# Mirrored filter rows by way of DRAM copies instead of flip products, no dummy root, first products from a constant

## The chip, the cores and the metric

The kernel runs on one core of a Trainium2 chip. The metric is the device time of one execution in microseconds (us). Inputs and output lie in DRAM; the work is done by TensorE (PE, matrix products, with its weight loads shown as PEld), VectorE (DVE), ScalarE (ACT), GpSimd (POOL, hardly used here) and SyncE (SP), which issues nearly all transfers (DMA).

## The reference

The input x (2048 x 512) goes two ways, and a gate mixes the results.

```python
x = A_x
g = _sigmoid((x * gate_w).sum(-1, keepdims=True))
a = irfft2(rfft2(x) * (w_r + 1j * w_i))          # 2048 x 512, filter 2048 x 257
h = layernorm(x)                                  # over the 512 columns
u = gelu(h^T @ w1 + b1)                           # 512 x 1792
b = (u @ w2 + b2)^T                               # 2048 x 512
return g * a + (1 - g) * b
```

`B_x` is not used. The part that the change is about is the product of the spectrum with the filter: the filter has 2048 rows (one for each frequency along the first axis) of 257 values, in a real half `A_w_r` and an imaginary half `A_w_i`. The kernel makes use of a symmetry between frequency k and frequency 2048 - k, so it needs each filter row together with its mirrored row in the same partition.

## The kernel before

**How the work is tiled.** The rows of x are held as 16 tiles of 128 rows (four blocks q, and within a block the row number modulo four, r). The transform is made of products with cosine and sine tables (L554 to L557 along the rows, L653 along the columns), with sums and differences on DVE between them (L566/L567, `radix4` at L585 to L601, L669 to L677). The spectrum lies in `X` and then in `B`, in two halves `lt`: the even frequencies (0) and the odd ones (1). It is multiplied by the filter (L820 to L842), taken back by the inverse products (L890 to L898, L967 to L970), and added to the other branch (L1017, L1024, L1030). The other branch is two dense products: L705 (with w1) sums over the 16 row tiles into one PSUM bank for each of 14 column tiles, gelu follows on ACT (L721), and L1011 (with w2) makes the 16 output tiles, each from 14 products. These 448 products of 512 columns are the bulk of PE's work; the short transform products stand between them.

**What sets the order.** Each piece of work is handed to a planner (`Plan`, L133) with its engine, its expected duration, a priority, the keys that it reads and writes, and, for loads, a size in bytes. `Plan.order` (L167) runs a small model of the engines and one model of the DMA (at most eight loads outstanding, 388 KB/us) and then emits all instructions in the order found. On the chip each engine works through its instructions strictly in this order, so a plan that expects a load too early makes its reader wait, and all that stands behind the reader on the same engine too. All transfers but five are issued by SP in one queue; each carries one of eight completion counters, in turn.

**The filter.** `W` (L325) holds, for each half (comp), each `lt` and four groups e, a forward row (s = 0) and its mirrored row (s = 1). `ld_W` (L433) loads one half in sixteen transfers: for `lt` = 1 the mirrored rows come by four transfers with a reversed source (L444), 128 rows each. For `lt` = 0 the rows that are to be mirrored are first loaded forward into a buffer `wt` (L439 to L442); PE then turns them over by products with a reversed unit matrix `flip` (`wf`, L757, and `wfn`, L767), and ACT copies the result into `W` (`wfe`, L761, and L770). Here is the core of the reversed load:

```python
for e in range(4):
    dma(W[:, 1, e, 1, 0:257], v[:, 3 - e, 3, :].rearrange("(o i) l -> o i l", o=4)[:, ::-1])
```

`wprep` (L775 to L782, DVE) halves one row of the filter and takes sums and differences of its end columns. It reads and writes all of `W`, so it runs after every load and every copy into it. `c0b` (L809 to L814) and the multiplications (L828) follow.

In SP's queue the order around the filter is: weights `wb` for column tiles 7 to 10, the tables, `ld_W(0)`, weights `wb` for tiles 11 to 13, `ld_W(1)`, then the w2 rows into `wa`.

**The start.** `alloc_first` (L308) allocates the buffers and clears a few of them on DVE, among them `warm`, the first 512 columns of `xp` (L317). PE multiplies this tile by itself ten times (`warm`, L356) ahead of the first real work. ACT takes the square root of a constant (`presq`, L361), which loads the table of the root. Then DVE takes the mean and variance of the first tile (L487, L488), ACT its root (L511), DVE the reciprocal and the normalised tile h (L516, L521), and PE starts with L705.

Of the kernel before, what the change touches and what calls it, by code (L numbers as in the profile page):

```python
# [264 lines left out]
def kernel(  # L265
# [23 lines left out]
    pool = ctx.enter_context(tc.tile_pool(name="sb", bufs=1))  # L289
    psum = ctx.enter_context(tc.tile_pool(name="ps", bufs=1, space=bass.MemoryType.PSUM))  # L290
# [17 lines left out]
    def alloc_first():  # L308
# [7 lines left out]
        t["warm"] = t["xp"][:, 0:D]  # L316
        V.memset(t["warm"], 0.0)  # L317
# [10 lines left out]
        t["wt"] = sb([P, 2, 4, WL], BF16, "wt")  # L328
# [12 lines left out]
    a0 = add("SP", 0.01, alloc_first, writes=["warm", "xs", "eps"], prio=-9)  # L341
# [11 lines left out]
    def warm():  # L353
        pw = ps([P, D], F32, "fa", 2)
        for _ in range(NWARM):
            T.matmul(pw[:], lhsT=t["warm"][:, 0:P], rhs=t["warm"], start=True, stop=True)  # L356
    NWARM = 10
    add("PE", 0.42 * NWARM, warm, reads=["warm", "xs"], writes=["warmed"], prio=-5, alloc=["fa"], free=["fa"])

    def presq():  # L360
        A.activation(t["ombb2"][:, 0:1], t["eps"][:], ActF.Sqrt, bias=t["eps"][:, 0:1], scale=1.0)  # L361
    add("ACT", 0.05, presq, reads=["eps"], writes=["omg"], prio=-5)


# [68 lines left out]
    def ld_W(comp):  # L433
# [3 lines left out]
        def emit():  # L437
            W, u = t["W"][:, comp], t["wt"][:, comp]
            dma(u[64:127, :, 0:257], v[65:128, :, 0, :])  # L439
            dma(u[0:64, :, 0:257], v[64:128, :, 2, :])  # L440
            dma(u[127:128, 0:2, 0:257], z[0:1, 1, 2:4, :])
            dma(u[127:128, 3:1:-1, 0:257], z[0:1, 0, 0:4:3, :])  # L442
            for e in range(4):
                dma(W[:, 1, e, 1, 0:257], v[:, 3 - e, 3, :].rearrange("(o i) l -> o i l", o=4)[:, ::-1])  # L444
# [4 lines left out]
            dma(W[0:1, 0, :, 0, 0:257].rearrange("w (u v) l -> w u v l", u=2), z[0:1, :, 0:2, :])  # L449
            dma(t["wn"][:, comp, 0:257], wsrc[comp][1024:1025, :])  # L450
        return emit

    for comp in range(2):
        add("SP", 12.3, ld_W(comp), writes=[("W", comp), ("wt", comp)], prio=17 + 8 * comp, nbytes=300000, after=[a0])
        if comp == 0:
            load_wb(1)
# [291 lines left out]

    for comp in range(2):
        for lt in (0,):  # L750
            for a in range(2):
                tag = ("fa", "fb")[a]

                def wf(comp=comp, lt=lt, a=a, tag=tag):
# [324 lines left out]
```

## Time and profile before

| what | us |
|---|---|
| median of three runs | 127.81 (127.77 to 128.35) |
| the profiled execution | 127.68 |
| its span | 125.9 |
| PE busy | 120.5 |
| DVE busy | 113.8 |
| ACT busy | 81.0 |
| first L705 product starts | 5.56 |
| filter loads issued by SP | 24.90 to 50.29 |
| flip products L757 | 38.7 to 53.6 |
| `wprep` (L777) starts | 57.46 |
| first L1011 product starts | 64.5 |

The profile shows one execution. Its span runs from the first to the last instruction; 1.78 us of the execution's time lie outside of it. The page gives, for each engine, its busy time and its share of the span, and below that the span in 40 slices of 3.15 us, a digit for each slice: 9 means busy for 90% or more. The groups give line, engine, operation, tiles and count, then the busy time in us and the mean duration of one in ns, then the idle time of that engine just before them and what ended it. In a timeline the first number is the start and the second the length; "SPq" is SP issuing a transfer. Products on PE overlap: the duration of one (379 ns for 512 columns) is longer than the distance from one start to the next (216 ns), and it is the distance that counts for a PE that is full. About two records in a hundred of PE's products are missing from the trace, so that a distance of twice 216 ns is mostly no gap.

### The profile page before, as it was taken

To read this page: it belongs to the slowest core of one execution; us is meant where nothing else is said; L and a number is where in the kernel's file an instruction comes from. 1 tells how busy PE (TensorE), PEld (TensorE's weight loads), DVE (VectorE), ACT (ScalarE), POOL (GpSimd) and SP (SyncE) were. 2 spreads that over 40 slices of the span, in tenths; PEclk is the share of its full clock that TensorE was granted. 3 is DMA by queue.
4 is the path that set the end of the run, shared out by engine and by line. 5 is a ranking of instruction groups with operands and counts; after the bars stand their busy time and mean duration, and the time that the engine had idled before them with its cause. 6 is when DMAs were issued, how large, how long until landed. Compare 5 with 4: busy or idle time off the path is not lost.

```text
span 125.9 us, 2138 instructions
## 1 busy us (share of the span) xinstructions
PE 120.5 (96%) x743; PEld 68.8 (55%) x756; DVE 113.8 (90%) x273; ACT 81.0 (64%) x165; POOL 0.2 (0%) x4
## 2 busy tenths in 40 slices
PE   6899999999999999999999999999999999999991
PEld 2344555555655476644445555555577767655590
DVE  2699999999999999999999999999988999999651
ACT  0973689699999999999420004722299999952200
POOL 0000000000000000000000000000000000000000
PEclk9999999999999999999999999999999999999999
DMA  1999999994459946799999900000000000006541
GB/s 57 305 371 358 382 365 358 348 315 86 117 119 288 268 86 162 210 413 411 410 408 407 389 25 0 5 0 0 3 0 0 0 5 0 0 21 229 200 180 44
DMA packets 18219, 23.12 MB, mean 184 GB/s; under 512 B 2190, under 2 KB 15904, under 8 KB 18208
## 3 DMA queue, kind: packets, MB, share of 16 engines
q1 hardware_dynamic: 17616, 22.36, 52.6%
q10 hardware_dynamic: 592, 0.62, 1.6%
q8 instruction: 6, 0.10, 0.3%
q14 instruction: 5, 0.04, 0.1%
HBM read 20.86 MB, written 2.10 MB: 182 GB/s over the span
## 4 chain that ended last, share of the span: by engine, by line
PE 73%; DMA 17%; SPq 7%; issue 1%; DVE 0%
PE acc L1011 32%; PE acc L705 20%; DMA wa<-in_B_w_dram 9%; SPq L306 7%; PE fb L1011 5%; DMA wt<-in_A_w_r_dram 5%; DMA x<-in_A_x_dram 3%; PE fb L653 2%; PE fa L653 2%; PE fa L890 2%; PE fb L890 1%; PE fb L705 1%; PE fa L967 1%; PE fb L967 1%; PE fa L1011 1%
## 5 line engine op out<-in xcount | busy, mean ns | idle before, releaser
L705 PE MATMUL acc<-h,wb 128*128 128x512 bf16 x108 | 25.9, 379 | 0.1
L1011 PE MATMUL acc<-gl,wb 128*128 128x512 bf16 (+1 forms) x94 | 23.9, 371 | 0.2
L1011 PE MATMUL acc<-gl,wa 128*128 128x512 bf16 (+1 forms) x97 | 23.8, 371 | 0.1
L1017 ACT ACTIVATE x<-acc,ombb,omg 128x512 bf16<-128x512 f32 x12 | 9.1, 782 | 21.2 <-PE acc L1011 21.2
L1011 PEld LDWEIGHTS <-wa 128*128 128x128 bf16 x126 | 13.5, 113 | 9.9
L1011 PEld LDWEIGHTS <-wb 128*128 128x128 bf16 x126 | 13.3, 113 | 9.3
L705 PE MATMUL acc<-h,wa 128*128 128x512 bf16 x62 | 17.3, 379 | 0.1
L705 PEld LDWEIGHTS <-wb 128*128 128x128 bf16 x112 | 10.7, 98 | 10.6
L705 PEld LDWEIGHTS <-wa 128*128 128x128 bf16 x112 | 10.3, 98 | 10.7 <-DMA wa<-in_B_w_dram 0.8
L487 DVE BATCH_NORM_STATS2 stats<-x 128x6 f32<-128x512 bf16 x14 | 9.5, 679 | 2.1 <-DMA x<-in_A_x_dram 2.0
L560 ACT CAST xp<-fa 128x512 bf16<-128x512 f32 x16 | 9.1, 581 | 1.8 <-PE fa L557 1.8
L735 ACT ACTIVATE x<-x 128x512 bf16<-128x512 bf16 x16 | 10.2, 691 | 0.0
L721 ACT ACTIVATE gl<-acc,b1f 128x512 bf16<-128x512 f32 x11 | 7.9, 718 | 3.2 <-PE acc L705 3.2
L705 PE MATMUL fb<-h,wa 128*128 128x512 bf16 x31 | 9.5, 379 | 0.1
L527 ACT ACTIVATE h<-x,nmr,rstd 128x512 bf16<-128x512 bf16 x11 | 8.4, 808 | 1.1 <-DMA wb<-in_B_w_dram 0.8
L705 PE MATMUL fa<-h,wa 128*128 128x512 bf16 x16 | 5.9, 378 | 0.7 <-DVE h L521 0.6
L653 PEld LDWEIGHTS <-X 128*128 128x128 bf16 x64 | 4.7, 98 | 2.1
L974 ACT ACTIVATE B<-fb,g 128x512 bf16<-128x512 f32 x8 | 5.7, 713 | 0.0
L974 ACT ACTIVATE B<-fa,g 128x512 bf16<-128x512 f32 x8 | 5.6, 705 | 0.1
L660 ACT CAST X<-fb 128x512 bf16<-128x512 f32 x8 | 5.1, 634 | 0.0
L660 ACT CAST X<-fa 128x512 bf16<-128x512 f32 x8 | 5.0, 620 | 0.0
L356 PE MATMUL fa<-xp 128*128 128x512 bf16 x10 | 3.8, 549 | 1.2 <-DVE xp L317 1.2
(169 smaller groups left out, 232.7 us busy)
## 6 DMA issues: line engine op xcount, KB each, us to landing
wb<-in_B_w_dram SPq DMA_DIRECT2D x11, 512.0 KB
wa<-in_B_w_dram SPq DMA_DIRECT2D x7, 512.0 KB
wa<-in_B_w_dram SPq DMA_DIRECT2D x2, 896.0 KB
wb<-in_B_w_dram SPq DMA_DIRECT2D x4, 384.0 KB
out_dram<-x SPq DMA_DIRECT2D x3, 512.0 KB
x<-in_A_x_dram SPq DMA_DIRECT2D x2, 512.0 KB
wa<-in_B_w_dram SPq DMA_DIRECT2D x2, 448.0 KB
rot<-dft_ti SPq DMA_DIRECT2D x1, 768.0 KB
```

Of the source, the lines that this page charges most:

```text
L306: (eng or nc.sync).dma_start(out=out_ap, in_=in_ap)
L487: V.bn_stats(out=t["stats"][:, j, :], in_=t["x"][:, j // 4, j % 4, :])
L527: add("ACT", 0.71, lambda j=j: A.activation(t["h"][:, j // 4, j % 4, :], t["x"][:, j // 4, j % 4, :], ActF.Identity, bias=t["nmr"][:, j:j ...
L560: add("ACT", act(512), lambda r=r, dq=dq: A.copy(xe(r)[:, :, :, dq, :], t["pa", r, dq][:]), reads=[("pa", r, dq)], writes=[("X", r, dq)], ...
L653: T.matmul(pb[:, k % 2, k // 2], lhsT=t["X"][:, lt, EX[e], c, k, :], rhs=tbl(k, c), start=True, stop=True)
L660: A.copy(t["X"][:, lt, EX[e]].rearrange("p c j l -> p (c j l)").rearrange("p (h c g b) -> p h c g b", h=2, c=2, b=2)[:, :, c], t["pb", lt, ...
L705: T.matmul(t["u", ft][:], lhsT=w[:, j // 4, j % 4, c * P:(c + 1) * P], rhs=t["h"][:, j // 4, j % 4, :], start=(j == jorder[0]), stop=(j == ...
L721: gelus.append(add("ACT", act(512, 1) , lambda ft=ft: A.activation(t["gl"][:, ft, :], t["u", ft][:], ActF.Gelu_apprx_tanh, bias=t["b1f"][: ...
L735: A.activation(t["x"][:, q, r, :], t["x"][:, q, r, :], ActF.Copy, accum_out=t["glog"][:, 4 * q + r:4 * q + r + 1])
L974: A.activation(eo_v(p)[:, n], t["i3", j][:], ActF.Copy, scale=t["g"][:, j:j + 1])
L1011: T.matmul(t["y", j, m][:, cs], lhsT=w[:, o, 512 * q + r:512 * q + 512:4], rhs=t["gl"][:, ft, cs], start=(ft == 0), stop=(ft == NFT - 1))
L1017: A.activation(tbuf(j).rearrange("p h d -> p (h d)"), t["y", j, 0][:], ActF.Identity, bias=t["ombb2"][:, j:j + 1], scale=t["omg"][:, j:j + 1])
```

## The change

Three things are changed.

1. The flip products, their evictions, the buffer `wt` and the loads into it are gone, and so are the four reversed loads of a half. Instead, for each half, two transfers copy the rows that are to be mirrored from DRAM to a DRAM buffer in reversed order (`ld_flip`: `fe` for the even, `fo` for the odd frequencies, 512 rows of 514 bytes each). Ten transfers load the forward rows and the few rows of partition 0 (`ld_nat`), and three fetch the mirrored rows from the DRAM buffers (`ld_mir`). The planner is told 1.1 us of issuing and 700000 bytes for `ld_flip`, 5.5 and 300000 for `ld_nat`, 1.6 and 500000 for `ld_mir`. `wprep` and the multiplications name the new key `("W~", comp)` of the fetched rows.
2. `presq`, the root of a constant, is gone. The first real root now carries the table load.
3. The ten first products read a constant tile of ones (one column, repeated) that POOL writes at the program's start, in place of the cleared piece of `xp`; the clear is gone, and the products wait for nothing on DVE.

The planner orders all work anew with these. SP's queue around the filter is now: tables, the four copies, the ten forward loads of half 0, the `wb` weights for tiles 11 to 13, the ten forward loads of half 1, the six fetches, then the w2 rows. `wprep` stands on DVE right behind L591 of the second half (`lt` = 1) and ahead of L669 and of L597/L598 of that half; before, thirty instructions stood between L591 and it.

```diff
+    dram = ctx.enter_context(tc.tile_pool(name="dram", bufs=1, space=bass.MemoryType.DRAM))
...
-        t["warm"] = t["xp"][:, 0:D]
-        V.memset(t["warm"], 0.0)
...
-        t["wt"] = sb([P, 2, 4, WL], BF16, "wt")
...
     def warm():
         pw = ps([P, D], F32, "fa", 2)
+        one = lambda n: nc.const_aps.tensor(1.0, [P, n], BF16)
         for _ in range(NWARM):
-            T.matmul(pw[:], lhsT=t["warm"][:, 0:P], rhs=t["warm"], start=True, stop=True)
+            T.matmul(pw[:], lhsT=one(P), rhs=one(D), start=True, stop=True)
     NWARM = 10
-    add("PE", 0.42 * NWARM, warm, reads=["warm", "xs"], writes=["warmed"], prio=-5, alloc=["fa"], free=["fa"])
-
-    def presq():
-        A.activation(t["ombb2"][:, 0:1], t["eps"][:], ActF.Sqrt, bias=t["eps"][:, 0:1], scale=1.0)
-    add("ACT", 0.05, presq, reads=["eps"], writes=["omg"], prio=-5)
+    add("PE", 0.42 * NWARM, warm, writes=["warmed"], prio=-5, alloc=["fa"], free=["fa"])
...
-    def ld_W(comp):
+    def ld_flip(comp):
+        ev = wsrc[comp].rearrange("(e m w) l -> w e m l", e=4, w=2)[0, :, P:2 * P, :]
+        od = wsrc[comp].rearrange("(g i k) l -> k g i l", i=32, k=4)[3]
+
+        def emit():
+            fe = t["fe", comp] = dram.tile([4, P, 257], BF16, tag=f"fe{comp}", name=f"fe{comp}")
+            fo = t["fo", comp] = dram.tile([16, 32, 257], BF16, tag=f"fo{comp}", name=f"fo{comp}")
+            dma(fe[:], ev[:, ::-1])
+            dma(fo[:], od[:, ::-1])
+        return emit
+
+    def ld_nat(comp):
         v = wsrc[comp].rearrange("(e c k) l -> c e k l", e=4, k=4)
         z = wsrc[comp].rearrange("(v u w) l -> w u v l", v=4, u=2)
 
         def emit():
-            W, u = t["W"][:, comp], t["wt"][:, comp]
-            dma(u[64:127, :, 0:257], v[65:128, :, 0, :])
-            dma(u[0:64, :, 0:257], v[64:128, :, 2, :])
-            dma(u[127:128, 0:2, 0:257], z[0:1, 1, 2:4, :])
-            dma(u[127:128, 3:1:-1, 0:257], z[0:1, 0, 0:4:3, :])
-            for e in range(4):
-                dma(W[:, 1, e, 1, 0:257], v[:, 3 - e, 3, :].rearrange("(o i) l -> o i l", o=4)[:, ::-1])
+            W = t["W"][:, comp]
             for o in range(4):
                 dma(W[32 * o:32 * o + 32, 1, :, 0, 0:257], v[96 - 32 * o:128 - 32 * o, :, 1, :])
             dma(W[1:64, 0, :, 0, 0:257], v[1:64, :, 0, :])
             dma(W[64:128, 0, :, 0, 0:257], v[0:64, :, 2, :])
             dma(W[0:1, 0, :, 0, 0:257].rearrange("w (u v) l -> w u v l", u=2), z[0:1, :, 0:2, :])
+            dma(W[0:1, 0, 0:2, 1, 0:257], z[0:1, 0, 0:4:3, :])
+            dma(W[0:1, 0, 3:1:-1, 1, 0:257], z[0:1, 1, 2:4, :])
             dma(t["wn"][:, comp, 0:257], wsrc[comp][1024:1025, :])
         return emit
 
+    def ld_mir(comp):
+        def emit():
+            W, fe, fo = t["W"][:, comp], t["fe", comp], t["fo", comp]
+            m = fe[:].rearrange("e (p two) l -> two p e l", two=2)
+            dma(W[:, 1, ::-1, 1, 0:257], fo[:].rearrange("(e o) i l -> (o i) e l", e=4))
+            dma(W[1:64, 0, ::-1, 1, 0:257], m[1, 0:63])
+            dma(W[64:128, 0, ::-1, 1, 0:257], m[0, 0:64])
+        return emit
+
+    FL = (16, 16.1)
     for comp in range(2):
-        add("SP", 12.3, ld_W(comp), writes=[("W", comp), ("wt", comp)], prio=17 + 8 * comp, nbytes=300000, after=[a0])
+        add("SP", 1.1, ld_flip(comp), writes=[("flp", comp)], prio=FL[comp], nbytes=700000, after=[a0])
+    for comp in range(2):
+        add("SP", 5.5, ld_nat(comp), writes=[("W", comp)], prio=17 + 8 * comp, nbytes=300000, after=[a0])
+        add("SP", 1.6, ld_mir(comp), reads=[("flp", comp)], writes=[("W~", comp)], prio=26 + comp, nbytes=500000)
...
-                def wf(comp=comp, lt=lt, a=a, tag=tag):
-                    pw = t["pw", comp, lt, a] = ps([P, 2, L], F32, tag, 2)
-                    for i in range(2):
-                        T.matmul(pw[:, i], lhsT=t["flip"][:], rhs=t["wt"][:, comp, 3 - 2 * a - i, 0:L], start=True, stop=True)
...
-                def wfe(comp=comp, lt=lt, a=a):
-                    A.copy(t["W"][:, comp, lt, 2 * a:2 * a + 2, 1, 0:L], t["pw", comp, lt, a][:])
...
-    def wfn():
...
-    add("DVE", 0.8, wprep, reads=[], writes=[("W", 0), ("W", 1), "wpm"] + wtk, prio=1)
+    add("DVE", 0.8, wprep, reads=[], writes=[("W", 0), ("W", 1), ("W~", 0), ("W~", 1), "wpm"], prio=1)
...
-            add("DVE", tt(4096), mul, reads=["xs", ("W", comp), ("W~", comp, lt)], writes=[("pp", "st")[comp]], prio=pr)
+            add("DVE", tt(4096), mul, reads=["xs", ("W", comp), ("W~", comp)], writes=[("pp", "st")[comp]], prio=pr)
```

More of the change, by code (lines that the diff above doesn't have):

```diff
@@ L339, in alloc_first @@
             t[name] = sb(shape, F32, name)
-    a0 = add("SP", 0.01, alloc_first, writes=["warm", "xs", "eps"], prio=-9)
+    a0 = add("SP", 0.01, alloc_first, writes=["xs", "eps"], prio=-9)
     def load(key, shape, dt, src, nbytes, prio=0.0):
@@ L747 @@
     add("SP", 0.2, ld_ti, writes=["ti"], prio=39, nbytes=754176, after=[pl.last_w["pa", r, dq] for r in range(4) for dq in range(4)])
[L749 to L752, printed above, removed]
-                def wf(comp=comp, lt=lt, a=a, tag=tag):
-                    pw = t["pw", comp, lt, a] = ps([P, 2, L], F32, tag, 2)
-                    for i in range(2):
-                        T.matmul(pw[:, i], lhsT=t["flip"][:], rhs=t["wt"][:, comp, 3 - 2 * a - i, 0:L], start=True, stop=True)
-                add("PE", mm(256, 256), wf, reads=[("wt", comp), "flip"], writes=[("pw", comp, lt, a)], prio=5, alloc=[tag])
-                def wfe(comp=comp, lt=lt, a=a):
-                    A.copy(t["W"][:, comp, lt, 2 * a:2 * a + 2, 1, 0:L], t["pw", comp, lt, a][:])
-                add("ACT", act(512), wfe, reads=[("pw", comp, lt, a)], writes=[("W~", comp, lt)], prio=3, free=[tag])
-    def wfn():
-        pw = t["pwn"] = ps([P, 4, 2], F32, "fa", 2)
-        for e in range(4):
-            T.matmul(pw[:, e], lhsT=t["flip"][:], rhs=t["wt"][:, :, 3 - e, 256], start=True, stop=True)
-    add("PE", mm(*[4] * 4), wfn, reads=[("wt", 0), ("wt", 1), "flip"], writes=["pwn"], prio=5, alloc=["fa"])
-    wtk = [("W~", comp, 0) for comp in range(2)]
-    add("ACT", 0.3, lambda: A.copy(t["W"][:, :, 0, :, 1, 256], t["pwn"][:].rearrange("p e k -> p k e")),
-        reads=["pwn"], writes=wtk, prio=3, free=["fa"])
     pbk = [("pb", lt, e, c) for lt in range(2) for e in range(4) for c in range(2)]
```

## The prediction

> **What bounds the kernel now.** I read the page's shares and slices first, then the groups kept apart by shape, the start, and the timelines of SP, DVE and PE around 24 to 58 us.
>
> ```profile
> PE 120.5 (96%) x743; PEld 68.8 (55%) x756; DVE 113.8 (90%) x273; ACT 81.0 (64%) x165; POOL 0.2 (0%) x4
> ...
> PE   6899999999999999999999999999999999999991
> ...
> DMA  1999999994459946799999900000000000006541
> ```
>
> PE is busy from the second slice to the last but one. From start to start its 512-column products take 0.216 us, the 256-column ones 0.109, the 128-column ones 0.056, and between 5.56 and 123 us no idle gap over 0.3 us is left. PE work is therefore the time; DVE is next, with one gap of 1.5 us near the end.
>
> ```profile
> L757 PE MATMUL fa<-wt,flip 128*128 128x256 bf16 x4 | 0.8, 272 | 0.0
> L757 PE MATMUL fb<-wt,flip 128*128 128x256 bf16 x4 | 0.8, 272 | 0.0
> L767 PE MATMUL fa<-wt,flip 128*128 128x2 bf16 x4 | 0.2, 165 | 0.0
> ```
>
> These are the products that go.
>
> ```profile
> 1.21 3.77 PE L356 MATMUL fa<-xp 128*128 128x512 bf16 x10 [1.21 <-DVE xp L317]
> ...
> 4.38 0.30 ACT L361 ACTIVATE ombb<-eps 128x1 f32<-128x1 f32 x1
> 4.58 0.28 ACT L511 ACTIVATE rstd<-mv,eps 128x1 f32<-128x1 f32 x1
> ...
> 5.56 0.38 PE L705 MATMUL fa<-h,wa 128*128 128x512 bf16 x1 [0.57 <-DVE h L521]
> ```
>
> The first real product waits for DVE, which waits for the first real root, which stands behind the dummy root.
>
> ```profile
> 24.90 2.56 SPq L306 DMA_DIRECT2D wt<-in_A_w_r_dram  x4
> 27.95 7.55 SPq L306 DMA_DIRECT2D W<-in_A_w_r_dram  x11
> ...
> 36.01 2.62 SPq L306 DMA_DIRECT2D wb<-in_B_w_dram  x4
> 38.68 2.54 SPq L306 DMA_DIRECT2D wt<-in_A_w_i_dram  x4
> 41.27 8.55 SPq L306 DMA_DIRECT2D W<-in_A_w_i_dram  x11
> 49.87 0.42 SPq L306 DMA_DIRECT2D wn<-in_A_w_i_dram  x1
> 50.40 3.30 SPq L306 DMA_DIRECT2D wa<-in_B_w_dram  x7
> ```
>
> SP takes about 0.57 us per issue, and no transfer is issued before the one eight places earlier has landed: issues at 27.95, 29.96, 44.00 and 45.57 follow such landings at 27.94, 29.94, 43.98 and 45.56. The filter is complete only at 52.0.
>
> ```profile
> 46.68 0.68 DVE L591 TENSOR_TENSOR X<-xp 128x1024 bf16<-128x1024 bf16 x1
> 47.55 0.69 DVE L669 TENSOR_TENSOR B<-X 128x1024 bf16<-128x1024 bf16 x1 [0.18 <-ACT X L660]
> ...
> 57.46 0.41 DVE L777 TENSOR_SCALAR W<-W 1x1028 bf16<-1x1028 bf16 x1
> ```
>
> Today `wprep` (L777 to L781), the first reader of the whole filter, runs at 57.46, over 5 us after the filter has landed.
>
> ```profile
> 50.83 0.39 PE L653 MATMUL fa<-tb,X 128*128 128x128 bf16 x4
> ```
>
> This is the first product that needs L597/L598 of the second half.
>
> **The change part by part.**
>
> *Products and evictions gone.* 8 x 0.109 + 4 x 0.02 = 0.95 us of PE, on the path as long as PE is full. ACT loses 4 x 0.65 + 0.34 = 2.9 us; PE and DVE cover it, so nothing. If ACT were the bound it would be a gain of up to 2.9.
>
> *Start.* Without the dummy root the real one starts when the statistics are ready (4.39) instead of 4.58: the table still loads at 3.08 to 4.36, since it stands ahead of the root's wait. Gain 0.15 to 0.19, say 0.15. The ten products begin some 0.3 us earlier (no wait for the clear); they end before the first h exists, so nothing, between -0.1 and +0.1. The lost DVE clear (0.27) falls into a 1.97 us wait.
>
> *The loads.* Per filter half, 16 transfers become 15: two that copy mirrored rows from DRAM into DRAM, ten forward ones, three that fetch the copies. The order is: four copies (both halves), ten forward loads, four weight loads (`wb`), ten forward, six fetches, then `w2`. Every packet is 514 bytes; their mean in the packet records of before is 36 ns (median 28).
>
> How many DMA engines carry a copy decides. The four odd mirrored loads of before (destination 128 partitions, source 4 reversed groups) each report only four engine ends, at 31.50, 32.77, 34.15 and 35.25 us for the last: 1.1 to 1.4 us for 32 packets, 34 to 43 ns each; in the second half 23 to 27. `fe` has the same shape (4 reversed groups), so I take four engines with 128 packets each; `fo` has 16 groups, so 16 engines with 32. No trace shows this with DRAM as destination.
>
> The Trainium skill's page DMA: Bandwidth & Descriptors (Why a DMA increments its semaphore by 16 and not by 1) says that the count is the largest number up to 16 that divides the slowest dimension of both sides, which gives 4 for fe; by it the spread-copy rival below falls away and the sum stays as it is.
>
> So the four engines get 128 + 32 + 128 + 32 = 320 packets. At 36 ns that is 11.5 us, from 28.9 (when these engines ran free before) to 40.4, landed at about 40.9. The eighth transfer behind the last copy, a two-packet forward load, is issued only then. Two small issues of 0.62 and the last of the ten follow, so `wb` starts at 42.8 instead of 36.01. The last `wb` took 9.5 us from the first issue in before (45.56), of which about 2 was backlog; I take 50.5. Behind that landing stand the eight last issues, 8 x 0.57 = 4.6, so the last fetch is issued by 55.1, and it lands 3.2 to 4.2 later (3.2 in before for the like load): **X = 58.7**, the landing of the last fetch.
>
> *The moved `wprep`.* In the changed order DVE runs it right behind L591 of the second half, at about 47.2, ahead of L669 and of L597/L598, which now queue behind a wait until X. DVE then needs 0.45 (wprep's tail) + 1.33 (L669 to L671) + 1.28 (L597, L598), and PE's product of 50.83 can start at X + 3.1. In the changed order four more 512-column products (0.87) stand before that product, and 0.51 of the removed ones stood behind it (0.44 ahead), so PE has 1.38 less to do after it. PE's end moves by X + 3.1 - 50.83 - 1.38 = X - 49.1. PE itself comes to it at 50.83 + 0.87 - 0.44 - 0.15 = 51.1; what PE and the start save before the wait only makes PE wait longer.
>
> X - 49.1 = 9.6. If X came before 47.2, no wait would be left and the change would give -0.95 - 0.15 = -1.1.
>
> *DVE lag.* DVE resumes X - 47.1 late, makes up 0.85 (wprep no longer at 57.46), and so lags PE by 1.15 more than before. In before, the inverse products start 0.2 to 0.4 us behind DVE's last writes (L601 ends at 92.94, its reader runs by 93.8). Between 0 and 1.15; I take 0.8.
>
> *The clock.* PE stands for X + 3.1 - 51.1 = 10.7 us. Before the first products the array was idle too, and they ran at 0.427 us until 4.17 us, 2.96 us long, at half rate: 1.48 us lost. Gaps of 0.3 to 0.7 us cost nothing of that kind. Between 0 and 1.5; the pause is nearer to the idle start, so 1.5.
>
> The Trainium skill's page TensorE: Matmul & The Clock Gate (Part 1: The HAM clock gate) gives a window of about 3.4 us both for falling to half rate and for rising again; an estimate by it is 1.7 us, and the sum would be 139.8. That the clock falls in a pause inside the kernel no trace here shows.
>
> *w2.* The first `wa` transfer moves from 50.40 to about 55.7, and seven at 1.28 us each land by 69; their first reader moves from 64.5 to about 75. Hidden; without the pause it would cost up to 5.
>
> **Sum.** 127.68 (the profiled execution: span 125.9 and 1.78 around it; median 127.81) + 9.6 + 0.8 + 1.5 = 139.6, say **139.5**.
>
> **Rivals.**
> - *The copies spread over 16 engines.* Then 4 x 32 packets take 4.6 us, the forward loads wait for nothing but SP, `wb` starts at about 37 and lands by 45.5, and X is 53.4: 127.68 + 4.3 = 132.0, up to 134.3 with lag and clock. For it: `fe`'s DRAM side is one unbroken run of rows. Against: the four-ended loads above. 18 in 100.
> - *DRAM to DRAM is slow.* Each packet crosses DRAM twice; at double the 40 ns the 320 packets take 25.6 us and X is 72.8: 127.68 + 23.7 + 2.3 = 153.7. 9 in 100.
> - *The fetches are in time, and it is faster.* From 30.7, when a slot for the third forward load comes free, 27 issues of 0.55 us and a landing of 2.6 give 48.2 if no copy and no `wb` holds a slot. X - 49.1 = -0.9: 126.6 to 126.8. It decides at X = 49.1. Against: the `wb` landings held SP at 44.00 and 45.57 already in before. 5 in 100, and 2 in 100 for an X so near 49 that nothing is seen.
> - The forecast, four engines at 23 to 50 ns: X 55 to 64, with or without the clock, 134.5 to 145: 66 in 100.
>
> **How the numbers follow.** 139.5 is the likeliest case's. 131.5 to 147 leaves out the faster and equal cases (7), the slow copies (9) and a little of the spread ones. Half a per cent is about what a measurement of this kernel tells from no change: faster 0.05, same 0.02, slower 0.93.
>
> **What would show it.** DVE idle at L767 to L771 of the changed file from 47 us on, ended by a transfer into W; copies into `fe` with four engine ends, 4 to 5 us apart; SP held at 31 to 41 us; PE idle from 51 us until 3 us after DVE resumes, then products at 0.427 us for about 3 us. The forecast is wrong if `fe` lands on 16 engines, if packets between DRAM and DRAM take far from 36 ns, or if the last fetch lands before 49 us.

## The result, and the profile after

The changed kernel takes **144.38 us** (median of six runs, 143.21 to 145.85) against 127.79 us in the six runs of the kernel before beside it: 1.126 times as long, 95% interval 1.121 to 1.131. Run again beside later experiments it took 146.01 us (ratio 1.140, interval 1.136 to 1.144), so differences of about 1% between runs of different groups mean nothing here. The medians are over all runs of a kernel; the ratios leave out those that took over 1.5% longer than its fastest.

The profiled execution took 145.41 us with a span of 143.5. The page of the changed kernel, shares and slices (each slice is now 3.59 us):

```profile
PE 123.5 (86%) x744; PEld 69.1 (48%) x744; DVE 113.4 (79%) x272; ACT 78.9 (55%) x159; POOL 0.2 (0%) x4
...
PE   7999999999999930001999999999999999999991
...
PEclk9999999999999996555599999999999999999999
DMA  3999999953954980799999574000000000004441
```

PE's row has a hole from 51 us on, and the clock's row is at half in it and behind it. The rest of PE's row is as full as before. The timeline of SP in the changed kernel (start and length of the issue, or of a run of issues with the waits between them):

```profile
25.18 0.75 SPq L307 DMA_DIRECT2D fe<-in_A_w_r_dram  x1
25.99 3.94 SPq L307 DMA_DIRECT2D fo<-in_A_w_r_dram  x1
29.98 0.84 SPq L307 DMA_DIRECT2D fe<-in_A_w_i_dram  x1
30.86 4.08 SPq L307 DMA_DIRECT2D fo<-in_A_w_i_dram  x1
34.98 7.99 SPq L307 DMA_DIRECT2D W<-in_A_w_r_dram  x9
...
43.47 2.62 SPq L307 DMA_DIRECT2D wb<-in_B_w_dram  x4
46.14 9.74 SPq L307 DMA_DIRECT2D W<-in_A_w_i_dram  x9
...
56.38 0.66 SPq L307 DMA_DIRECT2D W<-fo  x1
...
59.35 1.43 SPq L307 DMA_DIRECT2D W<-fe  x2
60.88 4.01 SPq L307 DMA_DIRECT2D wa<-in_B_w_dram  x7
```

The two copies into `fo` held SP for 4 us each. The first forward load went out at 34.98, where before had its first load into `W` at 27.95; the last fetch was issued at 60.19 and landed at 65.49. The timeline of DVE in the changed kernel, where `wprep` is L767 to L771, and below it that of PE:

```profile
46.88 0.68 DVE L605 TENSOR_TENSOR X<-xp 128x1024 bf16<-128x1024 bf16 x1
56.47 0.42 DVE L767 TENSOR_SCALAR W<-W 1x1028 bf16<-1x1028 bf16 x1 [8.90 <-issue]
62.72 0.19 DVE L770 TENSOR_TENSOR wpm<-W 128x16 f32<-128x16 bf16 x1 [5.83 <-DMA W<-fo]
65.57 0.19 DVE L771 TENSOR_TENSOR wpm<-W 128x16 f32<-128x16 bf16 x1 [2.66 <-DMA W<-fe]
...
66.94 0.68 DVE L611 TENSOR_TENSOR X<-st 128x1024 bf16<-128x1024 bf16 x1
```

```profile
50.39 1.24 PE L719 MATMUL acc<-h,wb 128*128 128x512 bf16 x5
67.68 0.61 PE L667 MATMUL fa<-tb,X 128*128 128x128 bf16 x4 [16.05 <-DVE X L611]
```

DVE finishes L605 at 47.6, meets `wprep`, and stands in it for 8.90 + 5.83 + 2.66 us until the last fetch is there. (The profile puts the first of the three down to "issue", that is to nothing that it shows; a load into `W` landed at 56.39, just before it ended.) L611, which PE wants at 51.6 us, is behind `wprep` in DVE's order, so PE stands for 16.05 us. This hole, and about 2 us for the half clock behind it, cover the 17.7 us between the two profiled executions: behind the hole PE runs without a gap of 0.25 us or more to the end.

### The profile page after: what moved, and what is told of

Its sections match the earlier page's. It is cut to its first block, busy times and chain, and to the rows that moved or that the text cites. A ratio compares the mean times of both kernels' runs of the same rounds, so it can differ in the third digit from the quotient of the medians.

```text
span 143.5 us, 2115 instructions
## 1 busy us (share of the span) xinstructions
PE 123.5 (86%) x744; PEld 69.1 (48%) x744; DVE 113.4 (79%) x272; ACT 78.9 (55%) x159; POOL 0.2 (0%) x4
## 4 chain that ended last, share of the span: by engine, by line
PE 51%; DMA 28%; SPq 17%; DVE 2%; issue 1%; DVEq 0%
PE acc L1001 28%; SPq L307 17%; PE acc L719 9%; DMA fe<-in_A_w_i_dram 8%; DMA wa<-in_B_w_dram 7%; DMA wb<-in_B_w_dram 6%; PE fb L1001 5%; DMA W<-fe 4%; DMA x<-in_A_x_dram 3%; PE fa L880 1%; PE fb L880 1%; PE fa L667 1%; PE fb L667 1%; PE fb L957 1%; PE fa L957 1%
## 5 line engine op out<-in xcount | busy, mean ns | idle before, releaser
L719 PE MATMUL acc<-h,wb 128*128 128x512 bf16 x112 | 26.8, 390 | 0.0
L1001 PE MATMUL acc<-gl,wb 128*128 128x512 bf16 (+1 forms) x98 | 24.2, 372 | 0.0
L1001 PE MATMUL acc<-gl,wa 128*128 128x512 bf16 (+1 forms) x98 | 23.8, 372 | 0.0
L1007 ACT ACTIVATE x<-acc,ombb,omg 128x512 bf16<-128x512 f32 x12 | 9.2, 788 | 20.2 <-PE acc L1001 20.2
L1001 PEld LDWEIGHTS <-wa 128*128 128x128 bf16 x126 | 13.4, 113 | 10.0
L719 PE MATMUL acc<-h,wa 128*128 128x512 bf16 x64 | 18.1, 388 | 0.0
L1001 PEld LDWEIGHTS <-wb 128*128 128x128 bf16 x126 | 13.3, 113 | 9.4
L667 PE MATMUL fa<-tb,X 128*128 128x128 bf16 x32 | 3.6, 242 | 16.1 <-DVE X L611 16.1
L719 PEld LDWEIGHTS <-wb 128*128 128x128 bf16 x112 | 11.0, 101 | 12.1 <-issue 0.8
L719 PEld LDWEIGHTS <-wa 128*128 128x128 bf16 x112 | 10.5, 99 | 10.9 <-issue 1.0
L749 ACT ACTIVATE x<-x 128x512 bf16<-128x512 bf16 x16 | 10.1, 666 | 0.0
L719 PE MATMUL fb<-h,wa 128*128 128x512 bf16 x32 | 9.7, 379 | 0.0
L767 DVE TENSOR_SCALAR W<-W 1x1028 bf16<-1x1028 bf16 x1 | 0.4, 420 | 8.9 <-issue 8.9
L719 PE MATMUL fa<-h,wa 128*128 128x512 bf16 x16 | 6.1, 392 | 0.2 <-DVE h L535 0.2
```

The lines of the kernel that those rows point to most:

```text
L667: T.matmul(pb[:, k % 2, k // 2], lhsT=t["X"][:, lt, EX[e], c, k, :], rhs=tbl(k, c), start=True, stop=True)
L719: T.matmul(t["u", ft][:], lhsT=w[:, j // 4, j % 4, c * P:(c + 1) * P], rhs=t["h"][:, j // 4, j % 4, :], start=(j == jorder[0]), stop=(j == ...
L749: A.activation(t["x"][:, q, r, :], t["x"][:, q, r, :], ActF.Copy, accum_out=t["glog"][:, 4 * q + r:4 * q + r + 1])
L1001: T.matmul(t["y", j, m][:, cs], lhsT=w[:, o, 512 * q + r:512 * q + 512:4], rhs=t["gl"][:, ft, cs], start=(ft == 0), stop=(ft == NFT - 1))
L1007: A.activation(tbuf(j).rearrange("p h d -> p (h d)"), t["y", j, 0][:], ActF.Identity, bias=t["ombb2"][:, j:j + 1], scale=t["omg"][:, j:j + 1])
```

## The experiments

In what follows X is the time at which the last fetch into `W` landed, read from the trace.

### Copies into fe on 16 engines (e1_spread)

```diff
-            dma(fe[:], ev[:, ::-1])
+            dma(fe[:].rearrange("e p l -> p e l"), ev.rearrange("e m l -> m e l"))
```

> The changed kernel, but the two copies into fe walk the 128 rows as their outer dimension and not the 4 groups, so that they can go over 16 DMA engines; bytes and packets (514 bytes) are the same. The reversal of these rows is left out, so fe holds them in forward order. Theory A (the copies make the last fetch late because four engines carry 320 packets each, and SP is held behind them): each copy into fe reports 16 engine ends and lands about 3 to 5 us after its issue, the long issues of the fo copies (3.94 and 4.08 us) fall below 1.5 us, the first forward load is issued by 29 (34.98 in the changed kernel), and the last fetch lands between 51 and 57 us (65.49). PE resumes 2.2 us after that landing, so the time is 145.4 less 8 to 14, less up to 2 for a clock that no longer falls: 130 to 137, I take 133. Rival B (packets from DRAM to DRAM, or SP writing 512 packets, are slow however many engines carry them): the last fetch stays at 63 or later and the time at 142 to 146.

Measured: 142.96 us (ratio 1.1215, interval 1.116 to 1.127), X = 61.65. Every copy now reported 16 engine ends, the issues of `fo` fell to 1.40 and 1.21 us and the first forward load went out at 29.65, much as theory A had it. But the two copies into `fe` landed 9.1 and 11.1 us after their issue, where theory A had 3 to 5, and the last copy landed at 39.58, only 1.9 us earlier than in the changed kernel (41.44). Rival B's time came true, if not quite its X of 63 or later. The reason is in the stretches of this run (for each stretch: its length, then busy time and count of PE, PEld, DVE, ACT, POOL, then the clock, the DMA engines' packet time as a share of the stretch, which passes 1 where packets of one engine overlap, and GB/s):

```profile
30.00:32.00 2.00, 2.00 (x13) 1.07 (x12) 2.00 (x4) 1.99 (x5) 0.00 (x0) 1.00 1.29 86
32.00:34.00 2.00, 2.00 (x18) 1.41 (x17) 2.00 (x4) 2.00 (x5) 0.00 (x0) 1.00 1.17 128
34.00:36.00 2.00, 2.00 (x14) 1.05 (x12) 2.00 (x5) 2.00 (x5) 0.00 (x0) 1.00 1.27 120
```

and the same of the changed kernel:

```profile
32.00:34.00 2.00, 2.00 (x19) 1.34 (x18) 2.00 (x3) 2.00 (x5) 0.00 (x0) 1.00 0.36 58
34.00:36.00 2.00, 2.00 (x16) 1.19 (x14) 2.00 (x5) 2.00 (x6) 0.00 (x0) 1.00 0.35 70
```

With four engines carrying `fe`, a third of the packet time of 16 engines is used in these four microseconds and the packets are shorter (514-byte packets: means of 36 to 53 ns for each microsecond): between the landing of the first `fe` at 34.76 and of the second at 40.95 each of the four engines took 128 + 32 rows, 39 ns each. With sixteen, all are full and still move only 86 to 128 GB/s: the packet records of this run have means of 67 to 146 ns for each microsecond from 30 to 38. That is more than in these four microseconds of the changed kernel, but not over the whole stretch of the copies: from 30 to 40 us the profile counts 121 GB/s in the changed kernel, with a packet time of 0.66 of the 16 engines, and 114 here, with 1.16. Four engines were a limit, but sixteen hardly carry more.

### wprep back behind the radix4 groups (e2_late), and both edits (e6_spread_late)

```diff
-    add("DVE", 0.8, wprep, reads=[], writes=[("W", 0), ("W", 1), ("W~", 0), ("W~", 1), "wpm"], prio=1)
+    add("DVE", 0.8, wprep, reads=[], writes=[("W", 0), ("W", 1), ("W~", 0), ("W~", 1), "wpm"], prio=1, after=[pl.last_w["B", 1, e] for e in range(4)])
```

> The changed kernel with wprep placed on DVE behind the radix4 groups of the second half (L669 to L677 of the file before), where it stood before the change at 57.5 us; the transfers are as in the changed kernel, but for what the planner moves. Theory A (what costs is where the wait for the last fetch, about 65.5 us, stands: ahead of the work on which PE's products of 51 us depend): PE's pause of 16.1 us and its half clock go. DVE waits at about 57 instead, for 8 us, and since DVE has only 1.5 us of idle time behind that place in the kernel before, PE loses most of these 8 us later: 127.7 less 1.1 plus 8.2 gives 134.8, range 132 to 138. Rival B (the late filter costs the same wherever DVE waits for it): 143 to 146. Rival C (DVE or PE has slack behind 57 us that takes the wait up): 126.5 to 130. The first weights of the w2 product land at about 66.6 where PE would want them at 63.5; a wait of up to 3 us at L1011 may show ahead of the one for DVE and lies inside it.

Measured: 145.31 us (ratio 1.1325, interval 1.125 to 1.140), no better than the changed kernel; X = 65.23. The time is rival B's, but not for its reason. PE's hole at 51 us is gone, and DVE waits in `wprep` from 57.5 to 65.3 as expected, but that wait is not what PE meets. The timeline of PE in this run (L1001 is the product with w2):

```profile
54.39 9.89 PE L719 MATMUL acc<-h,wb 128*128 128x512 bf16 x45 [0.68 <-DMA wb<-in_B_w_dram]
66.34 0.48 PE L1001 MATMUL acc<-gl,wa 128*128 128x512 bf16 x1 [2.06 <-DMA wa<-in_B_w_dram]
67.62 0.61 PE L1001 MATMUL acc<-gl,wa 128*128 128x512 bf16 x1 [0.80 <-DMA wa<-in_B_w_dram]
...
78.33 0.61 PE L1001 MATMUL acc<-gl,wb 128*128 128x512 bf16 x1 [3.08 <-DMA wb<-in_B_w_dram]
79.61 0.62 PE L1001 MATMUL acc<-gl,wb 128*128 128x512 bf16 x1 [0.67 <-DMA wb<-in_B_w_dram]
80.89 0.61 PE L1001 MATMUL acc<-gl,wb 128*128 128x512 bf16 x1 [0.66 <-DMA wb<-in_B_w_dram]
```

The w2 rows stand behind the fetches in SP's queue. From 66 to 81 us PE makes one product for each row block that lands, most of them 1.28 us apart, and the clock is at half from 66.5 to 83.6. The loss has moved from one reader to the next one of the same late queue. The expectation had a wait of 3 us here; it was wrong.

> Both edits together: the copies into fe on 16 engines (their reversal left out) and wprep behind the second half's radix4 groups. Theory A: the last fetch lands by 51 to 57 us, ahead of wprep at about 57, so no wait is left and the kernel shows what the dropped products (0.95 us) and the earlier root (0.15) are worth: 126.6, range 126.2 to 128.5, the upper part if the landing is nearer to 58. Rival B (the fetches stay late with spread copies): as with the late wprep alone, 132 to 138. Rival C (the dropped PE work is worth nothing because DVE sets the pace behind 57 us): 127.3 to 128.

Measured: 141.05 us (ratio 1.1027, interval 1.098 to 1.107); X = 61.40. Theory A failed: the fetches are late with spread copies too, as rival B has it, but the time is above rival B's 132 to 138. What sets it is again w2, whose third `wb` piece landed at 76.95 (80.84 in the run before).

### fo ahead of fe (e7_fofirst)

```diff
-            dma(fe[:], ev[:, ::-1])
             dma(fo[:], od[:, ::-1])
+            dma(fe[:], ev[:, ::-1])
```

> The changed kernel with the two copies of each half in the other order: fo (16 engines) ahead of fe (four). Theory A (SP is held in issuing a transfer when it stands behind a copy into fe, whose 128 packets for each of four engines are not yet taken): the first copy into fo is issued in under 1.5 us (3.94 us in the changed kernel), the second, which now stands behind fe, still takes 3 us or more, and so may a load that follows the second fe. Rival B (a transfer of 512 packets takes SP 4 us to issue by itself): both copies into fo take about 4 us. By either the four engines carry the same packets, so the last fetch lands within 2 us of 65.5 and the time is 142.5 to 146.

Measured: 143.82 us (ratio 1.1217, interval 1.1145 to 1.129), X = 63.33. The timeline of SP in this run:

```profile
24.61 1.18 SPq L307 DMA_DIRECT2D fo<-in_A_w_r_dram  x1
25.84 0.71 SPq L307 DMA_DIRECT2D fe<-in_A_w_r_dram  x1
26.60 3.42 SPq L307 DMA_DIRECT2D fo<-in_A_w_i_dram  x1
30.06 1.09 SPq L307 DMA_DIRECT2D fe<-in_A_w_i_dram  x1
```

The same copy of 512 rows takes 1.18 us to issue when nothing with four engines is ahead of it, and 3.42 behind a copy into `fe`. The first forward load, now behind the second `fe`, took 5.88. Theory A holds: it is the transfer ahead that holds SP. X is 2.2 us earlier than in the changed kernel's first profile, where both theories had it within 2.

### No copies (e4_nocopy), and no copies with wprep late (e10_nocopy_late)

```diff
-            dma(fe[:], ev[:, ::-1])
-            dma(fo[:], od[:, ::-1])
...
-            dma(W[:, 1, ::-1, 1, 0:257], fo[:].rearrange("(e o) i l -> (o i) e l", e=4))
-            dma(W[1:64, 0, ::-1, 1, 0:257], m[1, 0:63])
-            dma(W[64:128, 0, ::-1, 1, 0:257], m[0, 0:64])
+            dma(W[:, 1, ::-1, 1, 0:257], v[:, :, 3, :])
+            dma(W[1:64, 0, ::-1, 1, 0:257], v[65:128, :, 0, :])
+            dma(W[64:128, 0, ::-1, 1, 0:257], v[64:128, :, 2, :])
```

> The changed kernel without the four copies: the six fetches read forward rows straight from the filter, with the same row length and count, so the reversal of the mirrored rows is left out. Everything else stands in the same order. Theory C (the 2048 copied rows are extra transfer work that all later transfers pay for, about 6.6 ns for each row, or 13.5 us): the last fetch lands at 50 to 54 us (65.49 in the changed kernel), PE resumes 2.2 us later, its pause is under 5 us and the clock hardly falls: 128.5 to 132, I take 130. Rival D (the late fetches come from their place behind wb and the ten forward loads of the second half, with the eight outstanding transfers, and the copies add little): the last fetch at 57 or later, the time 136 or more.

Measured: 135.92 us (ratio 1.058, interval 1.049 to 1.066), X = 55.38. That lies between theories C and D: the copies are worth 10.1 us of X and 8.5 us of time (10.1 by the second measurement of the changed kernel), and the other 8 us of the loss are there without them. The timelines of SP and PE in this run:

```profile
33.40 2.61 SPq L307 DMA_DIRECT2D wb<-in_B_w_dram  x4
36.06 9.49 SPq L307 DMA_DIRECT2D W<-in_A_w_i_dram  x9
...
48.39 2.15 SPq L307 DMA_DIRECT2D W<-in_A_w_i_dram  x3
```

```profile
57.67 0.61 PE L663 MATMUL fa<-tb,X 128*128 128x128 bf16 x4 [5.98 <-DVE X L607]
```

From the first `wb` issue (33.40) to X it is 22.0 us, the same as in the changed kernel (43.47 to 65.49); before had 16.0 from its first `wb` issue (36.01) to the complete filter (52.0). Over the twelve profiles with the changed order this stretch takes 19.7 to 22.9 us (20.2 in the second profile of the changed kernel). So the stretch behind `wb` is 4 to 7 us longer than before, copies or not.

> No copies (the six fetches read forward rows straight from the filter, so the reversal is left out) and wprep behind the second half's radix4 groups. Theory J (what is left of the cost without copies, 8 us, is the last fetch at about 55.4 us under the moved wprep; and behind it the w2 weights): DVE meets wprep at about 57 with the filter in place and waits for nothing; the w2 weights are issued from 50.6 and their third later piece (wb) lands at about 71, where PE wants it at about 66, so that 3 to 6 us are lost there: 129 to 133, I take 131.5. Rival K (w2 is in time, and the dropped products and the earlier root show): 126.3 to 127.5. Rival L (without the copies the place of wprep makes no difference either): 135 to 137.

Measured: 135.00 us (ratio 1.0565, interval 1.053 to 1.060). DVE met `wprep` at 57.56 with the filter landed (55.10) and did not wait. The timeline of PE in this run (L997 is the product with w2):

```profile
63.74 1.67 PE L997 MATMUL acc<-gl,wa 128*128 128x512 bf16 x7
68.31 0.41 PE L997 MATMUL acc<-gl,wb 128*128 128x512 bf16 x1 [2.89 <-DMA wb<-in_B_w_dram]
69.70 0.62 PE L997 MATMUL acc<-gl,wb 128*128 128x512 bf16 x1 [0.98 <-DMA wb<-in_B_w_dram]
70.87 0.62 PE L997 MATMUL acc<-gl,wb 128*128 128x512 bf16 x1 [0.56 <-DMA wb<-in_B_w_dram]
```

Theory J named the right wait and the right pieces, but not the full price: 135 and not 131.5. From 65.3 to 71.3 us PE makes three products, which need 0.65 us, so 5.4 are lost; then the clock is at half until 75.8, which costs 2.3 more of PE's time. The time is rival L's. In the order of the changed file two tables (`ti`, `tg`) go ahead of the w2 rows called `wb`; before, four of these `wb` transfers went ahead of `ti`.

### Half the copies (e9_feonly)

```diff
-            dma(fo[:], od[:, ::-1])
...
+            for e in range(4):
+                dma(W[:, 1, e, 1, 0:257], v[:, 3 - e, 3, :].rearrange("(o i) l -> o i l", o=4)[:, ::-1])
```

> The changed kernel with half the copies: the odd mirrored rows (fo) are loaded in the way of the kernel before, by four reversed loads for each half, and only the even ones (fe, four engines, reversed) go by way of DRAM. Nothing is left out. Theory C (each copied row costs all that follows about 6.6 ns): 1024 rows less, so the last fetch lands about 6.7 us earlier than 65.49, at 57 to 61, and the time is 137 to 141, I take 139. Rival H (the four engines that carry fe set it, and fo rides along on the others): the last fetch at 63 or later, 142 to 146. Rival I (the fo copies are what holds SP and the rest, fe alone is carried beside other work): the last fetch by 55, 129 to 134.

Measured: 143.58 us (ratio 1.115, interval 1.106 to 1.125), X = 65.11: rival H. The run halves the copied rows but not the load of the four engines: the four reversed loads of a half bring 128 rows to each of them, where a spread `fo` brings 32. Until the first half is in, they carry 128 + 128 + 128 = 384 rows, and at the 36 ns that the packet records show that is 13.8 us, from 28 to 41.8; the last of the four reversed loads landed at 42.04. So theory C, a price for each copied row wherever it runs, is wrong.

### Rows in DRAM 576 bytes apart (e8_pad)

```diff
-            fe = t["fe", comp] = dram.tile([4, P, 257], BF16, tag=f"fe{comp}", name=f"fe{comp}")
-            fo = t["fo", comp] = dram.tile([16, 32, 257], BF16, tag=f"fo{comp}", name=f"fo{comp}")
-            dma(fe[:], ev[:, ::-1])
-            dma(fo[:], od[:, ::-1])
+            fe = t["fe", comp] = dram.tile([4, P, 288], BF16, tag=f"fe{comp}", name=f"fe{comp}")
+            fo = t["fo", comp] = dram.tile([16, 32, 288], BF16, tag=f"fo{comp}", name=f"fo{comp}")
+            dma(fe[:, :, 0:257].rearrange("e p l -> p e l"), ev.rearrange("e m l -> m e l"))
+            dma(fo[:, :, 0:257], od[:, ::-1])
```

> As the run with the copies into fe on 16 engines, but the rows in the DRAM buffers fe and fo lie 576 bytes apart and not 514 (they stay 514 bytes long; the reversal of the rows in fe is left out again). With the copies spread the 514-byte packets took 56 to 146 ns from 29 to 38 us, against 28 to 30 for those of the loads around them. Theory F (what is slow is writing rows to DRAM that begin at odd places and share their blocks with their neighbours): the packets fall below 50 ns, the last copy lands by 36 (39.6), the last fetch by 58 (61.65), and the time falls by 3 us or more, to 136 to 140. Rival G (a row that is read from DRAM and written to DRAM costs this much wherever it lies): packets and landings within 1 us of that run, and the time 142 to 144.

Measured: 138.98 us (ratio 1.082, interval 1.075 to 1.089), X = 58.29, last copy landed at 36.85. Against the run with spread copies that is 4 us less in time and 3.4 in X, with nothing changed but the distance between the rows. The same stretches as shown for that run:

```profile
30.00:32.00 2.00, 1.95 (x13) 1.03 (x13) 2.00 (x4) 1.99 (x5) 0.00 (x0) 1.00 1.00 175
32.00:34.00 2.00, 2.00 (x19) 1.35 (x17) 2.00 (x3) 2.00 (x4) 0.00 (x0) 1.00 1.12 175
34.00:36.00 2.00, 2.00 (x16) 1.24 (x15) 2.00 (x5) 2.00 (x6) 0.00 (x0) 1.00 0.92 138
```

The means of the packets fall to 42 to 55 ns between 30 and 36 us. Theory F is borne out in the time and in kind, though each of its other marks is just missed and the means stay above the 28 ns that is the median of the 514-byte packets in the kernel before. One run does not tell which side of the new distance helps, that no two rows share a block or that each begins at a multiple of 64 bytes. From the first fetch's issue to X the two runs take the same (8.8 and 8.7 us), so the gain lies in writing the copies and not in reading them back. The Trainium skill's page DMA: Bandwidth & Descriptors (How a descriptor splits into AXI transactions) says that a read must begin at a multiple of 256 bytes and pays for the bytes below its start. That rule is about reads, and 576 is no multiple of 256; what the run shows is on the writing side, and no run here tests the rule.

### Products in the pause (e3_warm and e3_again, after_again)

```diff
+                    if (lt, e, c) == (1, 1, 0):
+                        for _ in range(68):
+                            T.matmul(pb[:].rearrange("p a b s i -> p (a b s i)"), lhsT=nc.const_aps.tensor(1.0, [P, P], BF16), rhs=nc.const_aps.tensor(1.0, [P, D], BF16), start=True, stop=True)
```

> The changed kernel with 68 products of the tile of ones (0.216 us each, 14.7 in all) on PE ahead of the first product that it waits for at 51 us; their bank is written anew by the real products. They fill the pause, so that the clock record should stay full. Theory A (the pause lets the clock fall, and 3.93 us at half rate after it cost 1.97): the first real products behind the pause run at 0.109 us from start to start and not 0.214 (512 columns: 0.216 and not 0.43), and the time is 1.5 to 2 us less than that of the changed kernel, 142 to 143. Rival B (what PE loses there is made up later, or DVE is the pace behind the pause): 144 to 145. Rival C (the extra products end later than the data is there): 145 or more, with PE busy without a gap into the real products.

> The changed kernel itself once more, in the same runs as the next one, so that the two can be compared: 143.5 to 145.5.

> The products of ones in the pause a second time, beside the changed kernel. In the first profile the clock stayed full and the span ended 76.3 us after the last fetch landed, against 78.0 in the changed kernel, but the median of the runs did not fall. Theory A (the half clock after the pause costs about 1.7 us): 1 to 2 us less than the changed kernel beside it. Rival B (it costs nothing that lasts): within 0.5 of it. Rival C (the fetches land later when PE is kept busy, by as much as the clock gains): within 0.5 in the median, with the last fetch 1 us or more later in the profile.

Measured: 145.67 us in the first group (ratio 1.131, interval 1.120 to 1.142); in the second 145.51 (ratio 1.126, interval 1.122 to 1.131) beside 146.01 (1.140, 1.136 to 1.144) for the changed kernel itself. The clock's row of the first run, and PE around the end of the pause:

```profile
PEclk9999999999999999999999999999999999999999
```

```profile
51.27 15.04 PE L668 MATMUL fa<-const-bfloat16-1.0 128*128 128x512 bf16 x66
68.26 0.40 PE L670 MATMUL fa<-tb,X 128*128 128x128 bf16 x4 [1.95 <-DVE X L611]
```

Here the time of the profiled execution is 78.2 us above X (66.06); the changed kernel's are 79.9 and 80.5 above X (65.49 and 64.57). So the half clock is worth about 2 us, the size that theory A gave it, but its time of 142 to 143 was missed, and the medians are those of rivals B and C. X itself varies from run to run: in three of the second group's six runs the mean clock was below 1 (0.977 to 0.988) and these took 146.4 to 148.3 us. In the one of them that was profiled, X was 67.40, PE stood idle for 2.8 us behind the 68 products, the clock fell at 70.35 after all, and the time is again 79.9 above X. The three with a full clock took 143.3 to 144.7, and the second ratio rests on these alone. Whether X comes later when PE is busy was not settled, and rival C is not excluded.

### The small parts alone (e5_small)

```diff
-    def presq():
-        A.activation(t["ombb2"][:, 0:1], t["eps"][:], ActF.Sqrt, bias=t["eps"][:, 0:1], scale=1.0)
-    add("ACT", 0.05, presq, reads=["eps"], writes=["omg"], prio=-5)
...
+            T.matmul(pw[:], lhsT=one(P), rhs=one(D), start=True, stop=True)
```

> The kernel before with only the two small parts of the change: no root of a constant ahead of the first real one, and the ten first products from the tile of ones; the flip products and all filter loads stay. Theory A: the first real root starts 0.15 us earlier and with it all of PE: 0.1 to 0.2 us less than before, 127.6 to 127.7 where before has 127.8. Rival B (the first product waits for something else, the statistics or the first weights): no change within 0.1. Rival C (the table load of the root moves behind the statistics): 1.2 us more, 129.

Measured: 127.98 us beside 128.16 (ratio 1.0007, interval 0.998 to 1.003): no change. The start of this run:

```profile
4.39 0.30 ACT L507 ACTIVATE rstd<-mv,eps 128x1 f32<-128x1 f32 x1
...
4.92 0.41 DVE L517 TENSOR_SCALAR h<-x,mv,rstd 128x512 bf16<-128x512 bf16 x1
...
5.59 0.39 PE L701 MATMUL fa<-h,wa 128*128 128x512 bf16 x1 [0.85 <-DMA wa<-in_B_w_dram]
```

The real root starts 0.19 us earlier and h is there 0.17 earlier, but the first product now waits for the first w1 weights instead. This is rival B, by this profile; the interval of the ratio (0.3 us to either side) is too wide to tell the 0.15 of theory A from nothing. In the other profiles with this start the first real product began between 5.37 and 6.00 us. This is the only version here that is not slower than the kernel before; none is faster.

### What follows from X

| run | X | profiled time | time − X |
|---|---|---|---|
| changed kernel, twice | 65.49, 64.57 | 145.41, 145.10 | 79.9, 80.5 |
| fe on 16 engines | 61.65 | 142.23 | 80.6 |
| fo ahead of fe | 63.33 | 142.61 | 79.3 |
| fe alone copied | 65.11 | 144.91 | 79.8 |
| rows 576 bytes apart | 58.29 | 138.28 | 80.0 |
| no copies | 55.38 | 134.84 | 79.5 |
| pause filled, clock full | 66.06 | 144.23 | 78.2 |
| pause filled, clock fell | 67.40 | 147.25 | 79.9 |

As long as `wprep` stands where the change puts it, the time is X + 80 with any cause of X, and 78.2 above X in the one profile whose clock stayed full. Where it stands late, it is the landing of the third `wb` piece of w2 that counts: it landed at 80.84, 76.95 and 70.83 in the three late runs, and their profiled times (143.75, 140.16, 134.82) lie 62.9, 63.2 and 64.0 behind it. That landing in turn hangs on X (65.23, 61.40, 55.10): it came 15.6, 15.6 and 15.7 us later, with seven `wa` transfers, the two tables and two `wb` pieces in the queue between. This is why moving `wprep` gains so little: the time is X + 78.5, 78.8 and 79.7, whichever reader waits.

## Why the prediction was right, and where its sizes were off

The direction, the mechanism (DVE waits in `wprep` for the last fetch, and PE behind it) and the range held; the time was 4.9 us short of the median, and the range, 15.5 us wide, held although X came 6.8 us late. By its steps:

**Products and evictions (-0.95).** Nowhere seen by itself, since a wait follows in every run. The run without copies and with a late `wprep` comes nearest: 127.68 - 0.95 - 0.15, and the 7.7 us lost at w2, is 134.3 against 134.82 in its profile. That fits to half a microsecond, which is too coarse to tell a gain of 0.95 from half of it.

**Start (-0.15).** Not borne out: the table load stayed where the prediction had it and the root did start earlier, but the step did not name what is late next, the first w1 weights. In nine of the thirteen profiles with this start the first real product waits for them. In the changed kernel's first profile it waits for h and starts at 5.37, 0.19 earlier than before; there the pause at 51 us swallows the gain.

**Loads, up to the copies.** Right in size. Four engine ends for each copy into `fe`, sixteen for `fo`; 39 ns for a packet where 36 was taken; the last copy landed at 41.44 (predicted 40.9) and `wb` went out at 43.47 (42.8). That the size fits is in part luck: on sixteen engines, which the prediction took to be 7 us cheaper, the last copy landed at 39.58. Two readings were off without weight in the sum: the ends of the two copies into `fe` lie 6.2 us apart and not 4 to 5, and the second half's reversed loads of before give 23, 27 and 38 ns, not 23 to 27. Not foreseen: SP is held in the issues of `fo`. It costs little, since the four engines were busy until 41 us anyway: with the other order the holds lie elsewhere and the time is within the spread of the kernel's own runs.

**Loads, behind wb.** This is the term that failed: 15.9 us predicted from the first `wb` issue to X, 22.0 measured (20.2 in the second profile). Three parts of it were too small. The four `wb` took 11.2 us to land, 9.6 in the second profile (7.7 predicted by taking off 2 us of backlog from before's 9.5; without the copies, and so with less backlog, it was still 10.9). From that landing to the last fetch's issue it was 5.6 us (5.5) and not 4.6, because the fetches take 0.6 to 0.9 us each to issue where 0.57 was the mean. And the last fetch landed 5.3 us (5.0) after its issue and not 3.2 to 4.2: all six are issued within 3.8 us, and their 2040 packets keep the 16 engines busy from 58 to 65 us (packet time 0.98 of them), where before spread the same rows over both halves. X came at 65.49 instead of 58.7, +6.8.

**The moved wprep.** Right in kind: DVE waits in it, L611 and L612 queue behind it, PE stops at 51 us. PE resumed at X + 2.2 and not X + 3.1, since its first product waits for L611 only: -0.9. But the step reads as if the place of `wprep` were what costs the time, and that is not so: with `wprep` late the time is the same within 1 us, with copies or without, and 1.9 us less with the copies spread, because the w2 rows stand behind the fetches and make PE wait instead.

**w2.** "Hidden" held for the changed kernel. "Without the pause it would cost up to 5" was wrong: PE's waits at L719 and L1001 add up to 11.9 us with `wprep` late, with the half clock on top.

**DVE lag (0.8).** Nearly nothing: 127.68 + 65.49 - 49.1 - 0.9 + 2.0 for the clock leaves 0.2 of the 145.41.

**The clock (1.5).** Products ran at half rate from 67.68 to 71.61, 1.97 us lost; filling the pause gave 1.7 to 2.3 back. The clock fell at 54.55, 3 us after PE had stopped. The Trainium skill's page TensorE: Matmul & The Clock Gate (Part 1: The HAM clock gate) speaks of a window of 3413 ns that runs freely; the traces agree: full and half stretches last 47.79, 51.20, 61.44 and 6.83, 10.24, 13.65, 17.07 us, that is 14, 15, 18 and 2, 3, 4, 5 such windows. So the loss depends on where in a window PE resumes: after the long pause half rate lasted 2.9 us with `fo` ahead of `fe`, 3.4 without copies, 3.9 in the changed kernel and 5.4 in its second profile.

**The rivals.** "Copies spread over 16 engines" would have been priced wrong, at 132.0 to 134.3: made so, the kernel takes 142.96, since the 128 rows for each engine are then in at 39.6, 10.7 us after the 28.9 from which the prediction counts, and not 4.6. "DRAM to DRAM is slow" is false for four engines (39 ns) and half true for sixteen. "In time, and faster" did not occur; even without any copy X is 55.4, above the 49.1 at which it decides.

What stays open: why the four `wb` take 9.2 to 11.5 us to land in every run. The record shows where the time is: of the sixteen engine ends of the last one, fourteen came between 50.27 and 51.64 in the changed kernel and the other two at 52.52 and 54.62, and SP's next issue followed at 54.64; in the kernel before the last two came at 44.81 and 45.56, behind 43.73. So in these two runs it is one or two engines that are late, and what holds them is not known. Open too is what the dropped products are worth in an order in which both the filter and the w2 rows are in time. No such order was tried.

## What to carry to other kernels

When one queue feeds several late readers, follow a delay through the whole queue before naming its price: moving the first reader out of the way only hands the wait to the next one. Price transfers that land last by the packets issued together with them, not by one transfer's latency in a calmer stretch. A trip by way of DRAM saves at most about 1 us of products here and costs 2048 extra row transfers, so count rows, engines and the bytes between rows before replacing on-chip work by it.

## What the runs showed of the hardware that was not expected

- A transfer that follows a copy of 512 rows over four engines holds the issuing engine: 3.94 and 4.08 us in the changed kernel, 3.42 and 5.88 with the other order, 4.35 for a second `fe` behind the first, against 1.2 to 1.4 us for the same 512 rows with no such copy ahead.
- While copies of 514-byte rows from DRAM to DRAM ran over 16 engines, the 514-byte packets took 56 to 146 ns (means for each microsecond, 29 to 39 us) with rows 514 bytes apart, and 34 to 55 (29 to 37 us) with rows 576 apart; the last copy landed 2.7 us earlier.
- Spreading the same copies from four engines over sixteen brought the last landing only from 41.44 to 39.58.
- The clock also falls while PE works a little: with both edits it fell at 66.44, though no gap of PE in the 3.4 us before was longer than 0.87 us and PE was busy for 1.6 of them. With a late `wprep` alone and one product every 1.28 us it was at half from 66.5 to 83.6.
- At the start, the time from the first product to the full clock ranged from 2.6 to 6.0 us over the profiles of these kernels, with the first seven products at the same times, within 0.02 us, in all but the kernel before.
